# Attention over 512 heads: the row pitch of the spread V tile, 130 or 136 elements

## The chip, the cores and the metric

The kernel runs on one core of a Trainium2 chip. The metric is the device time of one execution in microseconds (us); before the change three runs gave 838.53, 837.74 and 838.30, a median of 838.3. A profiled execution of the same kernel took 837.31 us and has a span, from its first to its last instruction, of 835.6 us; all lines shown below come from it. The engines are named PE (TensorE's matmuls), PEld (TensorE's weight loads), ACT (ScalarE), DVE (VectorE), POOL (GpSimd) and SP (SyncE, which here issues all DMAs).

## The reference

Softmax attention without a mask, for 16 × 32 = 512 heads, each with 192 queries, 1024 keys and 128 dimensions, all in bf16:

```
scores = einsum("bhqd,bhkd->bhqk", q, k) * 128 ** -0.5
p      = softmax(scores, axis=-1)
out    = einsum("bhqk,bhkd->bhqd", p, v)
```

## The kernel before, in words

**Sets of four heads.** The 512 heads are worked on in 128 sets of four. A set is cut into three frames, so there are 384 frames. In frame `f = 3x + b` the tensor engine computes one third of the scores of set `x` (`qk(f)`, matmuls at L616) and then one third of the output of a set whose frame lies four back (`pv(f - LAG)`, matmuls at L638, `LAG` 4). That order, one score group and one PV group in turn, is written out in the loop at L666 to L671 and sets the beat of everything else.

**Scores.** The scores are made with keys on the partitions: a head's 1024 keys are 8 tiles of 128 keys, called `t`. Four heads sit at 32 partitions each and are multiplied side by side, one head on each quarter of the array's rows. A score group has 48, 64 or 48 matmuls. Its results lie in PSUM: head 0 in `f_s2`, heads 1 to 3 in `f_s0` or `f_s1` by turns.

**Exponential.** ACT reads a frame's scores from PSUM and writes exp(scale × score) as bf16 to `f_pt`, in two instructions: 512 wide for head 0 (L782) and 1536 wide for heads 1 to 3 (L785). No maximum is subtracted; at the end the row sums are tested for their range, and `_general_path` would do all of the work again if they lay outside. It is not executed here.

**V and its spread tile.** A set's V is loaded by one DMA of 1024 KB into `f_vs`, where each partition holds, for each of four heads, 8 rows of 128 elements without a gap. POOL copies them (function `spread`, L582, two copies per set with 16 rows each) into the tile `f_vp`, which has the shape 128 partitions × 2 sets × 32 rows × `VB` elements of bf16. Row `8·head + t` of a set is the right-hand side of the matmul for key tile `t` of that head. Only the first 128 elements of a row are written by the copy. Element 128 of each row is 1.0, since the whole tile is filled with ones at the start (L565). A matmul therefore reads 129 elements of a row, and the 129th column of its result is the row sum of the softmax:

```
return pe.matmul(
    O[m0: m0 + m, u, 0:129],
    pt[:, x % R, 2 * y + z, t * SQ + n0: t * SQ + n0 + m],
    vp[:, x % NVP, (2 * y + z) * T + t, 0:129],
```

The first operand after the output, a slice of 64 columns of `f_pt`, is loaded as weights; the row of `f_vp` streams through. Elements 129 up to `VB` of a row are never read.

**The order in a PV group.** A PV group has 32 matmuls: 16 pairs (`z` = 0, 1) that work side by side, the first on columns 0 to 63 of the array, the second on columns 64 to 127. The two of a pair read rows that are 8 rows apart, those of two neighbouring heads with the same `t`. In the first and second group of a set (`i` = 0, 1) there are two blocks, and each goes through `t` = 0 to 7, one row per pair. In the third group (`i` = 2) `t` is the outer loop and two output blocks (`u` = 0, 1) the inner one: each row is read by two pairs in succession, with other weights.

**Normalizing and storing.** After each PV group DVE takes the reciprocal of the row sums (L722) and multiplies the outputs by them into `f_ob` (L726). The next PV group waits for that, as there is one output bank, `f_o`. SP stores two sets with one DMA.

**K and Q.** K comes with a DMA of 1024 KB per set into `f_kn` (five buffers); DVE turns it in 32×32 blocks into `f_kx` (L701, three pieces per set), POOL reorders it into `f_kt` (L573), from which the score matmuls load their weights. Q comes with 192 KB per set and is turned by DVE (L710). On DVE these turns stand in one queue with the reciprocals and scalings: a K piece is turned five frames ahead of its use, right after the scaling of a frame.

**The loads.** SP issues per turn of its loop V of a set three ahead, K and Q of a set five ahead, and every second turn a store. A K load waits until DVE has turned the set that was in that buffer (L502), a V load until the PV groups of the set that was in that buffer are far enough (L516).

Of the kernel before, what the change touches and what calls it, by code (L numbers as in the profile page):

```python
# [408 lines left out]
def _attention_kernel(nc, q, k, v, out):  # L409
# [12 lines left out]
    NKN, NVS, NKT, NVP = 5, 5, 2, 2  # L422
    GQ = 2
    NSO = 3
    VB = 130

    qf = q.rearrange("b h s d -> (b h) s d")
    kf = k.rearrange("b h s d -> (b h) s d")
# [6 lines left out]
    with ExitStack() as outer:  # L435
# [27 lines left out]
        with ExitStack() as es:  # L463
            def sb(name, shape, dt):
                return es.enter_context(nc.sbuf_tensor(name, shape, dt))
# [13 lines left out]
            vs = sb("f_vs", [128, NVS, 4, T * D], BF16)  # L479
            vp = sb("f_vp", [128, NVP, 4 * T, VB], BF16)  # L480
            pt = sb("f_pt", [128, R, 4, T * SQ], BF16)
# [308 lines left out]
def bass_standalone__mha_softmax__near_ridge_kernel(  # L790
    nc: bass.Bass,
    q: bass.AP,
    k: bass.AP,
    v: bass.AP,
    out: bass.AP,
):
    _attention_kernel(nc, q, k, v, out)
# [28 lines left out]
```

## Time and profile before

| | us | share of the span of 835.6 us |
|---|---|---|
| PE busy (32926 matmuls) | 818.2 | 98% |
| PE, PV matmuls into `f_o` (L638, 12336) | 434.3 | |
| PE, score matmuls (L616, 20480) | 421.6 | |
| PEld busy | 726.0 | 87% |
| ACT busy | 748.6 | 90% |
| DVE busy | 599.3 | 72% |
| POOL busy | 550.0 | 66% |
| POOL, V copies (L582, 256 of 1.043 us) | 259.5 | |
| DMA, time of all packets over 16 engines | | 99.5% |

A group's busy time is the time in which at least one of its instructions was at work. Matmuls overlap, so the two groups of PE add up to more than PE's own total, and the mean of one matmul (222 ns in L638) is its way from start to end, not its share of the time; what a matmul costs is the distance from its start to the next one's. A row of the page ends with the idle time of the engine just ahead of the group's instructions and what ended most of it. In a list of waits the three numbers are the total in us, how many there were, and the longest. The line of GB/s has one number for each fortieth of the span.

The tile `f_vp` takes 2 × 32 × 130 × 2 = 16640 bytes of each partition. [...]

### The profile page before, as it was taken

What the parts mean: (1) busy time and instruction counts of PE and PEld (TensorE: products, weight loads), DVE (VectorE), ACT (ScalarE), POOL (GpSimd) and SP (SyncE); (2) the same over time, 40 slices, a digit from 0 to 9 for tenths busy, and PEclk for the clock granted to TensorE, in tenths of its full rate; (3) what the DMA queues carried; (4) which work ended last, traced back from release to release, by engine and by line L of the source; (5) the groups of instructions that cost most, each with busy time, mean ns of one, the idle gap of its engine ahead of it and who ended that gap; (6) DMA issues with size and microseconds to landing.
All of it is one profiled execution on the core that took longest, in us unless ns stands there. A gap on an engine that the chain in (4) does not pass through costs nothing. (4 is left out here: it accounts for less than half of the span.)

```text
span 835.6 us, 71554 instructions
## 1 busy us (share of the span) xinstructions
PE 818.2 (98%) x32926; PEld 726.0 (87%) x32926; DVE 599.3 (72%) x1288; ACT 748.6 (90%) x770; POOL 550.0 (66%) x646
## 2 busy tenths in 40 slices
PE   7899999999999999999999999999999999999995
PEld 5788888888888888888888888888888888888885
DVE  5577777777777777777777777777777777777763
ACT  5799999999999999999999999999999999999994
POOL 6566666666766766766766666666666666666670
PEclk9999999999999999999999999999999999999999
DMA  8999999999999999999999999999999999999941
GB/s 323 398 404 400 406 403 403 404 403 406 403 406 403 401 397 401 394 399 394 392 404 397 389 403 399 390 400 398 393 401 396 397 397 396 395 393 394 395 161 43
DMA packets 139213, 319.21 MB, mean 382 GB/s; under 512 B 7200, under 2 KB 57376, under 8 KB 122912
## 3 DMA queue, kind: packets, MB, share of 16 engines
q1 hardware_dynamic: 139168, 318.80, 99.5%
q14 instruction: 39, 0.32, 0.1%
q8 instruction: 6, 0.10, 0.1%
HBM read 293.60 MB, written 25.17 MB: 381 GB/s over the span
## 5 line engine op out<-in xcount | busy, mean ns | idle before, releaser
L785 ACT ACTIVATE f_pt<-f_s 128x1536 bf16<-128x1536 f32 x384 | 554.6, 1444 | 1.8 <-PE f_o L638 1.8
L573 POOL COPY f_kt<-f_kx 128x768 uint32<-128x768 uint32 (+1 forms) x384 | 293.8, 784 | 265.7 <-DVE f_kx L701 140.2
L638 PE MATMUL f_o<-f_vp,f_pt 128*64 128x129 bf16 x12336 | 434.3, 222 | 1.8 <-issue 1.8
L616 PE MATMUL f_s<-f_qt,f_kt 32*128 32x192 bf16 (+2 forms) x20480 | 421.6, 226 | 5.9 <-issue 3.4
L638 PEld LDWEIGHTS f_o<-f_vp,f_pt 128*64 128x64 bf16 x12336 | 373.9, 110 | 53.7 <-issue 23.5
L616 PEld LDWEIGHTS f_s<-f_qt,f_kt 32*128 32x128 bf16 x20480 | 347.6, 92 | 43.0 <-issue 6.5
L701 DVE STREAM_TRANSPOSE f_kx<-f_kn 128x768 uint32<-128x768 uint32 (+1 forms) x384 | 333.8, 870 | 10.1 <-DMA f_kn<-in_k_dram 10.1
L782 ACT ACTIVATE f_pt<-f_s 128x512 bf16<-128x512 f32 x384 | 229.3, 597 | 72.6 <-PE f_s L616 37.8
L582 POOL COPY f_vp<-f_vs 128x1024 uint32<-128x1024 uint32 x256 | 259.5, 1043 | 4.5 <-PE f_o L638 4.5
L722 DVE RECIPROCAL f_rinv<-f_o 128x2 f32<-128x2 f32 x381 | 65.0, 171 | 202.6 <-PE f_o L638 202.6
L726 DVE TENSOR_TENSOR f_ob<-f_o,f_rinv 128x256 bf16<-128x256 f32 x381 | 161.6, 424 | 13.3 <-DVE f_rinv L722 0.3
L710 DVE STREAM_TRANSPOSE f_qt<-f_qn 128x384 uint32<-128x384 uint32 x128 | 73.0, 570 | 0.0
L663 PE MATMUL f_o<-f_ones 128*128 128x512 bf16 x12 | 5.1, 610 | 1.1 <-POOL f_ones L564 1.1
L663 PEld LDWEIGHTS f_o<-f_ones 128*128 128x128 bf16 x12 | 1.7, 145 | 3.8 <-issue 2.7
L682 DVE MEMSET f_pt<- 128x3072 uint32 x1 | 2.6, 2618 | 1.5 <-PEq L811 1.5
L565 POOL MEMSET f_vp<- 128x4160 uint32 x1 | 3.6, 3569 | 0.0
L638 PE MATMUL f_s<-f_vp,f_pt 128*64 128x129 bf16 x96 | 3.1, 220 | 0.3 <-PEq L599 0.3
L638 PEld LDWEIGHTS f_s<-f_vp,f_pt 128*64 128x64 bf16 x96 | 2.9, 110 | 0.4 <-issue 0.4
L774 ACT ACTIVATE f_pt<-f_ones 128x3072 f32<-128x3072 bf16 x1 | 2.8, 2762 | 0.0
L774 ACT ACT_TABLE_LOAD x1 | 1.3, 1283 | 0.8 <-PEq L811 0.8
L722 DVE RECIPROCAL f_rinv<-f_s 128x2 f32<-128x2 f32 x3 | 0.5, 171 | 1.4 <-PE f_s L638 1.4
L676 PE MATMUL f_o<-f_bad,f_ones 128*1 128x1 bf16 x1 | 0.2, 165 | 1.3 <-DVEq L766 1.3
(13 smaller groups left out, 5.3 us busy)
## 6 DMA issues: line engine op xcount, KB each, us to landing
f_vs<-in_v_dram SPq DMA_DIRECT2D x128, 1024.0 KB, 10.5
f_kn<-in_k_dram SPq DMA_DIRECT2D x127, 1024.0 KB, 12.6
f_qn<-in_q_dram SPq DMA_DIRECT2D x128, 192.0 KB, 11.5
out_dram<-f_ob SPq DMA_DIRECT2D x63, 384.0 KB, 12.9
f_kn<-in_k_dram SPq DMA_DIRECT2D x1, 640.0 KB, 6.9
f_kn<-in_k_dram SPq DMA_DIRECT2D x1, 384.0 KB, 3.9
out_dram<-f_ob SPq DMA_DIRECT2D x2, 192.0 KB, 2.1
```

What stands on the lines that cost most here:

```text
L573: gp.tensor_copy(kt[:, x % NKT].bitcast(U32).rearrange("p U (j s u) c -> p U j s (u c)", s=2, u=2)[:, lo:hi], kx[:, x % 2].rearrange("p (U ...
L582: gp.tensor_copy(vp[:, x % NVP, 2 * T * i: 2 * T * i + 2 * T, 0:D].bitcast(U32), vs[:, x % NVS, 2 * i: 2 * i + 2, :].rearrange("p a (t d) ...
L616: ins = pe.matmul(S[:, c0: c0 + n1 - n0], kt[r, x % NKT, 2 * t + h, :, c], qt[r, x % R, h, n0:n1, c], start=w == 0 and g == 0, stop=w == 3 ...
L638: return pe.matmul(O[m0: m0 + m, u, 0:129], pt[:, x % R, 2 * y + z, t * SQ + n0: t * SQ + n0 + m], vp[:, x % NVP, (2 * y + z) * T + t, 0:129],
L663: pe.matmul(o_ps[:].rearrange("p a b -> p (a b)"), ones[:], ones[:].unsqueeze(1).to_broadcast([128, 4, 128]), start=True, stop=True)
L701: dve.transpose(kx[:, x % 2].rearrange("p (U s j u) -> p s u U j", s=2, j=32, u=2)[:, :, :, lo:hi], kn[:, x % NKN].rearrange("p (s u U i) ...
L710: dve.transpose(qt[:, x % R].bitcast(U32).rearrange("p b (y j u) c -> p u y b (j c)", y=3, u=2), qn[:, x % NKN].rearrange("p (u y b i) -> ...
L722: dve.reciprocal(ri, O[:, :, 128]).then_inc(s_rc, 1)
L726: dve.tensor_tensor(ob[:, so, 6 * a + 2 * w: 6 * a + 2 * w + 2, :], O[:, :, 0:128], ri.unsqueeze(2).to_broadcast([128, 2, D]), ALU.mult,). ...
L774: act.activation(pt[:, 1].rearrange("p a c -> p (a c)").bitcast(F32), ones[:, 0:1].to_broadcast([128, 2 * T * SQ]), ACT_FN.Copy).then_inc( ...
L782: act.activation(pt[:, x % R, 0, c], s1_ps[:], ACT_FN.Exp, scale=scale).then_inc(s_e1, 1)
L785: act.activation(pt[:, x % R, 1:4, c], s3_ps[f % 2][:], ACT_FN.Exp, scale=scale).then_inc(s_e3, 1)
```

## The change

`VB`, the number of elements from one row of `f_vp` to the next, goes from 130 to 136, that is, from 260 to 272 bytes. The 129 elements that are written and read in each row stay the same, as do the number and order of all instructions, their waits and the DMAs. The fill at the start covers 4352 words of 32 bits for each partition in place of 4160, and the tile takes 17408 bytes in place of 16640; `f_pt`, `f_ob` and the tiles after them lie 768 bytes higher.

```
     NKN, NVS, NKT, NVP = 5, 5, 2, 2
     GQ = 2
     NSO = 3
-    VB = 130
+    VB = 136
```

More of the change, by code (lines that the diff above doesn't have):

```diff
@@ L424, in _attention_kernel @@
     NSO = 3
-    VB = 130
+    VB = 136
     qf = q.rearrange("b h s d -> (b h) s d")
```

## Prediction, made before the changed kernel ran

> **What bounds the kernel now.** I read the page's engine totals first, then the costliest groups, then one stretch of the timeline, then the waits, and at the end the transfers.
>
> ```profile
> PE 818.2 (98%) x32926; PEld 726.0 (87%) x32926; DVE 599.3 (72%) x1288; ACT 748.6 (90%) x770; POOL 550.0 (66%) x646
> ...
> L573 POOL COPY f_kt<-f_kx 128x768 uint32<-128x768 uint32 (+1 forms) x384 | 293.8, 784 | 265.7 <-DVE f_kx L701 140.2
> L638 PE MATMUL f_o<-f_vp,f_pt 128*64 128x129 bf16 x12336 | 434.3, 222 | 1.8 <-issue 1.8
> L616 PE MATMUL f_s<-f_qt,f_kt 32*128 32x192 bf16 (+2 forms) x20480 | 421.6, 226 | 5.9 <-issue 3.4
> ...
> L582 POOL COPY f_vp<-f_vs 128x1024 uint32<-128x1024 uint32 x256 | 259.5, 1043 | 4.5 <-PE f_o L638 4.5
> ```
>
> The matmuls that read the spread V tile (L638) and those of the scores (L616) fill the span between them, with 1.8 and 5.9 us of idle time in front; POOL, which writes the tile, idles 265.7 us at L573 alone. The timeline of the matmuls alone shows the beat:
>
> ```profile
> 400.29 1.13 PE L638 MATMUL f_o<-f_vp,f_pt 128*64 128x129 bf16 x32
> 401.36 1.10 PE L616 MATMUL f_s<-f_qt,f_kt 32*128 32x192 bf16 x48
> 402.38 1.11 PE L638 MATMUL f_o<-f_vp,f_pt 128*64 128x129 bf16 x32
> 403.43 1.09 PE L616 MATMUL f_s<-f_qt,f_kt 32*128 32x192 bf16 x64
> 404.50 1.13 PE L638 MATMUL f_o<-f_vp,f_pt 128*64 128x129 bf16 x32
> 405.56 1.09 PE L616 MATMUL f_s<-f_qt,f_kt 32*128 32x128 bf16 x48
> ```
>
> Columns: start, length. A set of four heads is three score groups and three PV groups of 32, with no gap. By the first score matmul of each set, sets 3 to 127 follow each other every 6.295 and 6.285 us in turn, one exception at 6.371. Such a regular beat means that TensorE waits for nobody. So what a PV matmul costs is what counts.
>
> The waits and the transfers show who is next:
>
> ```profile
> DVE f_kx L701 <- DMA f_kn<-in_k_dram: 10.1, 5, 2.9
> ...
> GB/s 323 398 404 400 406 403 403 404 403 406 403 406 403 401 397 401 394 399 394 392 404 397 389 403 399 390 400 398 393 401 396 397 397 396 395 393 394 395 161 43
> ...
> q1 hardware_dynamic: 139168, 318.80, 99.5%
> ...
> f_kn<-in_k_dram SPq DMA_DIRECT2D x127, 1024.0 KB, 12.6
> ```
>
> Nobody waits for K after the start-up (five waits), yet the DMA engines are loaded 99.5% of the span, and a K transfer takes 12.6 us from issue to landing, two beats: there is always a backlog. DMA is a second bound just behind TensorE.
>
> [...] The trace has 56 ns for some pairs of PV matmuls (two run side by side) and 59 to 60 for the rest. [...] but the trace does follow the offset, below. [...] the trace moved 404 GB/s for 200 us[...].
>
> **The change, part by part.**
>
> *PV matmuls.* Row r of the tile starts at 260·r bytes now: at offset 0, 4, 8, 12 within 16 bytes as r mod 4 goes 0 to 3. Rows are numbered head·8 + t, so t = 0 and t = 4 begin at a multiple of 16 today. That is a test inside the trace. From the starts of single matmuls in 367 full PV groups between 20 and 800 us, the median from one pair to the next, in ns:
>
> ```
> pair of the group         1  2  3  4  5  6  7  8  9 10 11 12 13 14
> first group  (t = pair mod 8)  59 59 59 56 59 59 60 56 60 59 59 56 59 59
> second group (t = pair mod 8)  61 60 60 56 60 59 60 56 60 59 60 56 60 59
> third group  (t = pair div 2)  57 61 56 60 56 60 56 56 57 61 56 60 56 60
> ```
>
> (Pairs 0 and 15 border on the score groups, a switch of 80 to 185 ns.) In the first two groups exactly the pairs with t = 0 or 4 take 56 ns. In the third, where each row is read by two pairs in succession, the first reading takes 60 when the row is off the 16-byte grid and 56 when it is on it (pair 8, t = 4), the second reading 56 always. Offsets in the weights don't give this pattern: the first group's blocks start their weights 128 bytes apart and both show it. Why a second reading is free I can't say. With a pitch of 272 bytes all rows are on the grid, at 0, 16, 32 or 48 within 64 bytes, and rows at each of these places take 56 ns today.
>
> Saving: group one has 12 off-grid pairs at a mean of 59.6 against 56.3: 12 × 3.3 = 39.6 ns. Group two, 59.8: 12 × 3.5 = 42. Group three, six first readings at 60.0 against 55.9: 6 × 4.1 = 24.6. Sum 106 ns per set, from 6.290 to 6.184 us. Sets 0 to 2 are paced by K's and V's arrival at the start (starts at 6.9, 17.0, 30.2 us), so I count 125 sets: 13.2 us.
>
> *POOL's copies.* 256 at 1043 ns, now written at another pitch. The K copies fall from 859 to 635 ns over 256 words, 0.875 ns a word and 187 fixed; the V copy at that fixed part has (1043 − 187)/1024 = 0.836 ns a word. It is already the cheaper per word, so I take no change. Bounds: −100 to +100 ns each; POOL is idle a third of the time, and 200 ns per set more vanishes in L573's waits.
>
> *The first fill* (L565) grows from 4160 to 4352 words: 3569 × 4352/4160 = 3734, +165 ns. It ends at 4.5 us, POOL's next work starts at 5.80 and waits for DVE: hidden, nothing.
>
> *Later tiles* move up by 768 bytes, a multiple of 256: nothing. No instruction, wait or transfer is added.
>
> *ACT and DVE at the shorter beat.* ACT starts its 512-wide Exp at the end of each score group, the 1536-wide one 494 ns later, which takes 1444: 1.94 us out of a beat of 2.06. It fits. DVE idles 0.36 to 0.61 us ahead of each reciprocal; it fits.
>
> *DMA at the shorter beat.* A set moves 2.49 MB (K and V 1024 KB each, Q and output 192 each). Until 280 us the DMA ran at 404 GB/s, 6.16 us per set. What counts is the last of the 16 engines to land each K: set 12 at 77.2, 36 at 226.4, 126 at 791.0 us: 6.217 us per set, then 6.273. DVE's turn of a K starts this long after its landing: 5.98 us for set 12, 7.75 (36), 7.93 (60), 9.33 (126). TensorE will ask every 6.184. At set 12 about 0.8 us of slack has been eaten: 5.2 left. If the late engine keeps 6.217, the deficit over 114 sets is 3.8 us, less than the slack: nothing is lost. At 6.273 throughout, or as recorded, DVE begins to wait at about set 80 and the gain ends 3.3 to 3.5 us short. I take the middle, 6.245: 114 × 0.061 = 7.0 against 5.2, so 1.8 us is lost. DVE runs reciprocals and scalings in the same queue as the K turns, so its wait holds back the next PV group.
>
> Sum against the profiled span: 835.6 − 13.2 + 1.8 = 824.2. The other runs have a median of 838.3 (837.74 to 838.53); the same 11.4 off gives 826.9.
>
> **Rivals.** About 0.2% is what a measurement of this kernel tells from no change.
>
> 1. *DMA never binds.* Late landing engine at 6.217 or better; for it speaks 404 GB/s when all engines were loaded. Full saving: 838.3 − 13.2 = 825.1. Against: a backlog to the end, and the last engine at 6.273.
> 2. *DMA binds harder.* One slow engine of the recorded kind from the start, or transfers slowed by more overlap: half of the saving, 830 to 835. For: the rate falls from 404 to 396. Against: K's slack grew all the way.
> 3. *It doesn't do what it says.* The rhythm belongs to t, not to the address, and stays: 838.3. For: the free second reading, which I can't explain. Against: pair 8 of the third group.
> 4. *Slower.* The two matmuls of a pair read rows 8 apart, 2080 bytes today, 2176 after, a multiple of 128. If the streams then collide, each pair costs what an off-grid one does now. The fast ones of today (four pairs in groups one and two, nine in three) lose 3.4 to 4 ns: about 60 ns per set, 128 × 0.060 = 7.7: 846.0. It decides once a mean pair costs more than today's 58.6 ns. For: no such distance is in the trace. Against: weights read at a distance of 3072 bytes, also a multiple of 128, with nothing to see.
>
> **How the numbers follow.** Main case, saving with DMA taking back part, 825.9 to 829.5: 0.50. Rival 1, 823.5 to 825.9: 0.24. Rival 2: 0.11. Rival 3: 0.06. Rival 4: 0.09. Main and rival 1 hold 0.74; the range goes to 831 to take in part of rival 2: 823.5 to 831. Faster 0.50 + 0.24 + 0.11 = 0.85 and a little for a partial effect in rival 3: 0.86; same 0.05; slower 0.09.
>
> **What would show it.** Right: pairs of L638 at 56 ns for every t; PV groups of about 1.02 us from first start to next score group; sets at 6.18 us; more "DVE f_kx L701 <- DMA" waits, in the last third. POOL's L582 stays at 1043 ns. Wrong: 59 to 60 ns pairs still there (rival 3), or everywhere (rival 4); K waits from the first third on (rival 2).

## The result, and the profile after

The changed kernel takes 830.84 us (median of four runs, 829.76 to 831.68), the kernel before 838.02 on the same occasions (836.79 to 838.53): a ratio of 0.9916, 95% interval 0.9897 to 0.9934. So 7.2 us were gained, where 11.4 had been forecast (826.9 us; range 823.5 to 831.0).

The page of the changed kernel, the lines that answer to those shown of before, and the first fill:

```profile
PE 810.1 (98%) x32926; PEld 718.3 (87%) x32926; DVE 601.8 (73%) x1288; ACT 748.5 (90%) x770; POOL 550.9 (66%) x646
...
GB/s 323 399 403 399 406 403 401 406 403 402 405 403 404 402 400 389 399 382 374 398 400 398 376 399 395 388 400 405 387 383 399 406 397 397 387 393 405 399 323 46
...
q1 hardware_dynamic: 139168, 318.80, 100.6%
...
L638 PE MATMUL f_o<-f_vp,f_pt 128*64 128x129 bf16 x12336 | 424.9, 222 | 5.2 <-issue 3.3
...
L582 POOL COPY f_vp<-f_vs 128x1024 uint32<-128x1024 uint32 x256 | 259.9, 1044 | 5.9 <-PE f_o L638 5.5
...
L565 POOL MEMSET f_vp<- 128x4352 uint32 x1 | 3.7, 3730 | 0.0
...
f_kn<-in_k_dram SPq DMA_DIRECT2D x127, 1024.0 KB, 14.2
```

L638 is busy 9.4 us less (434.3 before), with the same mean of 222 ns: what shrank is the distance between starts. POOL's copy is unchanged. The timeline shows where the time came from:

```profile
301.41 1.10 PE L638 MATMUL f_o<-f_vp,f_pt 128*64 128x129 bf16 x32
302.44 1.10 PE L616 MATMUL f_s<-f_qt,f_kt 32*128 32x128 bf16 x48
303.47 1.10 PE L638 MATMUL f_o<-f_vp,f_pt 128*64 128x129 bf16 x32
304.50 1.09 PE L616 MATMUL f_s<-f_qt,f_kt 32*128 32x192 bf16 x48
305.52 1.10 PE L638 MATMUL f_o<-f_vp,f_pt 128*64 128x129 bf16 x32
306.55 0.49 PE L616 MATMUL f_s<-f_qt,f_kt 32*128 32x192 bf16 x20
```

From the start of a PV group to the next score group it is now 1.03 us in all three groups; before it was 1.06, 1.06 and 1.05 (medians 1059, 1063 and 1045 ns, now 1030 each). The starts of single pairs follow each other every 56 to 57 ns for every `t`. Sets follow each other every 6.20 and 6.22 us by turns, 6.210 on average against 6.290. That holds up to set 82. Then every second set is longer. The waits show two that were not there before:

```profile
DVE f_kx L701 <- DMA f_kn<-in_k_dram: 30.2, 42, 3.6
...
DVE f_ob L726 <- DMA out_dram<-f_ob: 7.1, 22, 0.9
```

DVE now waits 37 times for K after 480 us, and 22 times for an older store of the outputs, whose buffer it needs. One place, DVE's timeline first and TensorE's below it:

```profile
600.11 0.98 DVE L701 STREAM_TRANSPOSE f_kx<-f_kn 128x768 uint32<-128x768 uint32 x1 [0.20 <-DMA f_kn<-in_k_dram]
601.39 0.17 DVE L722 RECIPROCAL f_rinv<-f_o 128x2 f32<-128x2 f32 x1 [0.30 <-PE f_o L638]
602.42 0.42 DVE L726 TENSOR_TENSOR f_ob<-f_o,f_rinv 128x256 bf16<-128x256 f32 x1 [0.86 <-DMA out_dram<-f_ob]
```

```profile
601.29 1.10 PE L616 MATMUL f_s<-f_qt,f_kt 32*128 32x128 bf16 x48
602.99 1.10 PE L638 MATMUL f_o<-f_vp,f_pt 128*64 128x129 bf16 x32 [0.61 <-PEq L599]
```

K comes 0.20 us late, and the reciprocal behind it still starts on time: DVE had 0.30 us to spare. The scaling, however, waits 0.86 us for the store, and the PV group that needs its output bank starts 0.61 us late. Over the sets from 78 on, the odd ones, in which a store's buffer is taken up again, exceed the average of the sets before by 3.4 us in total, the even ones by 0.1. From set 76 on, 19 PV groups start more than 40 ns later after their score group than in the sets before, 3.2 us in all, and each of them follows a scaling that waited for a store. So it is the stores' late landing that costs TensorE time here, not K's.

### The profile page after: what moved, and what is told of

It reads as the page before. It is cut to its first block, busy times and chain, and to the rows that moved or that the text cites. A ratio compares the mean times of both kernels' runs of the same rounds, so it can differ in the third digit from the quotient of the medians.

```text
span 829.9 us, 71554 instructions
## 1 busy us (share of the span) xinstructions
PE 810.1 (98%) x32926; PEld 718.3 (87%) x32926; DVE 601.8 (73%) x1288; ACT 748.5 (90%) x770; POOL 550.9 (66%) x646
## 5 line engine op out<-in xcount | busy, mean ns | idle before, releaser
L785 ACT ACTIVATE f_pt<-f_s 128x1536 bf16<-128x1536 f32 x384 | 554.5, 1444 | 3.4 <-PE f_o L638 3.4
L638 PE MATMUL f_o<-f_vp,f_pt 128*64 128x129 bf16 x12336 | 424.9, 222 | 5.2 <-issue 3.3
L638 PEld LDWEIGHTS f_o<-f_vp,f_pt 128*64 128x64 bf16 x12336 | 366.1, 110 | 57.6 <-issue 28.3
L582 POOL COPY f_vp<-f_vs 128x1024 uint32<-128x1024 uint32 x256 | 259.9, 1044 | 5.9 <-PE f_o L638 5.5
L565 POOL MEMSET f_vp<- 128x4352 uint32 x1 | 3.7, 3730 | 0.0
L638 PE MATMUL f_s<-f_vp,f_pt 128*64 128x129 bf16 x96 | 3.1, 220 | 0.3 <-PEq L599 0.3
L638 PEld LDWEIGHTS f_s<-f_vp,f_pt 128*64 128x64 bf16 x96 | 2.8, 110 | 0.5 <-issue 0.5
## 6 DMA issues: line engine op xcount, KB each, us to landing
f_kn<-in_k_dram SPq DMA_DIRECT2D x127, 1024.0 KB, 14.2
f_qn<-in_q_dram SPq DMA_DIRECT2D x128, 192.0 KB, 12.9
out_dram<-f_ob SPq DMA_DIRECT2D x63, 384.0 KB, 13.8
```

What stands on the lines that cost most here:

```text
L582: gp.tensor_copy(vp[:, x % NVP, 2 * T * i: 2 * T * i + 2 * T, 0:D].bitcast(U32), vs[:, x % NVS, 2 * i: 2 * i + 2, :].rearrange("p a (t d) ...
L638: return pe.matmul(O[m0: m0 + m, u, 0:129], pt[:, x % R, 2 * y + z, t * SQ + n0: t * SQ + n0 + m], vp[:, x % NVP, (2 * y + z) * T + t, 0:129],
L785: act.activation(pt[:, x % R, 1:4, c], s3_ps[f % 2][:], ACT_FN.Exp, scale=scale).then_inc(s_e3, 1)
```

## The experiments

The kernel before, measured beside each, had medians of 837.45 to 838.15 us; the ratios are against it.

**1. All rows off the grid, at one place** (shift2). Pitch 272 bytes, but the row's data lie 4 bytes further on:

```
-    vp[:, x % NVP, 2 * T * i: 2 * T * i + 2 * T, 0:D]          # written by spread
+    vp[:, x % NVP, 2 * T * i: 2 * T * i + 2 * T, 2:2 + D]
-    vp[:, x % NVP, (2 * y + z) * T + t, 0:129],                # read by pv
+    vp[:, x % NVP, (2 * y + z) * T + t, 2:131],
```

> Pitch 272 bytes as in the changed kernel, but each row's 129 elements lie at elements 2 to 130 of its slot, so that every row begins 4 bytes past a multiple of 16. Theory A (what counts is whether a row begins on the 16-byte grid): all first readings of a row are off the grid, 40 pairs of each set of 48 against 30 in the kernel with pitch 260; at the 2.6 ns per such pair that the two traces give ((6.290 - 6.210) us / 30) a set takes 6.316 us and the kernel 841 us, up to 845 if it is 3.4 ns. Pairs in the trace at 59 to 60 ns for every t. Theory B (what counts is the distance between rows, 272 in place of 260 bytes, not where they begin): pairs at 57 ns and about 831 us, as in the changed kernel.

Measured 832.25 us, ratio 0.9935 (0.9914 to 0.9956). PV groups of 1030 ns, pairs at 56 to 57 ns, sets of 6.214 us up to set 77: TensorE works as in the changed kernel. Theory A, on which the forecast rested, is false: a row that begins off a multiple of 16 bytes costs nothing, as long as all do so by the same amount. POOL's copies took 1057 ns in place of 1044.

**2. Two places by turns, 0 and 8** (pitch132).

```
-    VB = 136
+    VB = 132
```

> Pitch of 132 elements, 264 bytes: rows with even t begin at a multiple of 16, rows with odd t 8 bytes past one. Theory A: 8 + 8 + 4 = 20 off-grid first readings per set in place of 30, 10 fewer: 26 ns per set less than the kernel with pitch 260, 6.263 us per set, 834.7 us; pairs at 57 ns for even t and 59 to 60 for odd t. That K arrives late costs little at this beat, at most 1 us. Theory B (distance): some other value for all t alike.

Measured 833.83 us, ratio 0.9961 (0.9949 to 0.9973). Even `t` 56 ns, odd `t` 59 to 60, groups of 1045, 1045 and 1038 ns, sets of 6.248 us. In the third group the first reading of an odd row took 61 ns, all else 56. By itself this would speak for theory A; with run 1 it says that a row's place counts only together with the row read before it.

**3 and 4. Half of the V traffic** (half_v_130 and half_v_136), on the kernels before and after:

```
-    vs[:, x % NVS, :, :],
-    vf[4 * x:4 * x + 4].rearrange("a (m t) d -> m a (t d)", t=T),
+    vs[:, x % NVS, 0:2, :],
+    vf[4 * x:4 * x + 2].rearrange("a (m t) d -> m a (t d)", t=T),
...
-    vs[:, x % NVS, 2 * i: 2 * i + 2, :]
+    vs[:, x % NVS, 0:2, :]
```

> The kernel before (pitch 130 elements) with half of the V traffic: only heads 0 and 1 of each set are loaded, and their V is used for heads 2 and 3 as well, so heads 2 and 3 get the wrong V. All engine instructions stay. Theory A' (TensorE sets the time of the kernel before, DMA does not): 838.0 us, within 0.2%, apart from up to 2 us gained in the first sets, which wait for their loads. Rival (DMA holds back the kernel before already): below 835 us.

> The changed kernel (pitch 136 elements) with the same half of the V traffic (heads 2 and 3 get the V of heads 0 and 1). Theory A' (in the changed kernel the late arrival of K takes back part of TensorE's saving): sets of 6.210 us from start to end, no wait for K after the start-up, 10.0 us below the same kernel with pitch 130 (125 sets of 0.080 us), so about 828 us or a little less. Rival (the rest of the forecast saving is missing on TensorE alone, and the waits for K cost nothing): 830.8 us, as in the changed kernel.

Measured 837.59 us with pitch 130 (ratio 0.9995, 0.9983 to 1.0006) and 827.40 with pitch 136 (0.9880, 0.9863 to 0.9897). The waits of the latter for loads and the beginning of its transfer line:

```profile
DVE f_kx L701 <- DMA f_kn<-in_k_dram: 7.7, 5, 3.2
...
f_kn<-in_k_dram SPq DMA_DIRECT2D x127, 1024.0 KB, 6.9
```

K lands in 6.9 us in place of 14.2, only the five waits of the start-up are left, none for a store, and the sets stay at 6.211 us to the end. So the kernel before is set by TensorE alone; the layout is worth 10.2 us on TensorE (837.59 − 827.40); and late transfers take back 3.4 of them (830.84 − 827.40; these two were measured on different occasions, and the trace gives 3.5, below).

**5. Another order of the rows, no other address** (t_order_130), on the kernel before:

```
-    for t in range(T):
+    for t in (0, 4, 1, 5, 2, 6, 3, 7):       # first and second group only
```

> The kernel before, pitch 130 elements, but in the first and second PV group of a set the key tiles are taken in the order 0, 4, 1, 5, 2, 6, 3, 7, so that each second row begins at the same place within 16 bytes as the one before it; no address in the tile is changed. Theory C (a pair costs more when its row begins at another place within 16 bytes than the row read before it, and not at place 0): 3 of 8 pairs of a block cost 59 to 60 ns in place of 6, the second reading of a place is as cheap as in the third group; 12 slow pairs fewer per set, 12 x 3.3 = 40 ns, sets of 6.25 us, 838 - 125 x 0.040 = 833 us. Theory A (a row off the 16-byte grid always costs more): 6 of 8 stay slow, 838 us.

Measured 834.59 us, ratio 0.9957 (0.9938 to 0.9976). Groups one and two fall to 1032 ns, the third stays at 1044; sets take 6.227 us until stores and K come late, which is below the 6.25 expected. Of the six steps up in a group only three or four are slow, at 58 to 60 ns. With the old pitch the order alone gives most of the gain on TensorE. Theory A is refuted a second time.

**6. The order turned round** (t_down_130), on the kernel before:

```
-    for t in range(T):
+    for t in range(T - 1, -1, -1):           # first and second group only; the accumulation
+                                             # then starts at t = T - 1 and stops at t = 0
```

> The kernel before, pitch 130 elements, but in the first and second PV group of a set the key tiles are taken from 7 down to 0: the places within 16 bytes go 12, 8, 4, 0, 12 and so on, a change at each pair as before, but down three times of four. No address in the tile is changed. Theory C1 (only a step up costs, 3 to 6 ns, and pairs can't go below 56 to 57 ns on average): groups one and two take 1.03 us as with pitch 136, sets of 6.22 to 6.23 us, 832 to 835 us with the waits for K. Theory C2 (any change to a place other than 0 costs): three of four pairs stay at 59 to 60 ns, groups of 1.06 us, sets of 6.29 us, 838 us.

Measured 832.48 us, ratio 0.9931 (0.9913 to 0.9948). Every pair reads another place than the pair before, but groups one and two take 1032 to 1033 ns, as theory C1 says. In their timeline they are the second and third L638 line, after one of the third group:

```profile
300.76 1.11 PE L638 MATMUL f_o<-f_vp,f_pt 128*64 128x129 bf16 x32
301.81 1.10 PE L616 MATMUL f_s<-f_qt,f_kt 32*128 32x192 bf16 x64
302.89 1.10 PE L638 MATMUL f_o<-f_vp,f_pt 128*64 128x129 bf16 x32
303.92 1.09 PE L616 MATMUL f_s<-f_qt,f_kt 32*128 32x128 bf16 x48
304.94 1.10 PE L638 MATMUL f_o<-f_vp,f_pt 128*64 128x129 bf16 x32
305.97 1.10 PE L616 MATMUL f_s<-f_qt,f_kt 32*128 32x192 bf16 x48
```

1.05 us for the third group, whose order was left, 1.03 for the other two. Within these only the pairs at a step up, from place 0 to 12, are slow, 60 to 61 ns: `t` = 3, which comes after `t` = 4, in each block, and `t` = 7, which opens the second block after `t` = 0. The steps down, from 12 to 8, 8 to 4 and 4 to 0, show 56 to 57 ns.

**7. Two places by turns, 0 and 4** (two_places), with a pitch on the grid:

```
-    vp = sb("f_vp", [128, NVP, 4 * T, VB], BF16)
+    vp = sb("f_vp", [128, NVP, 2 * T, 288], BF16)              # two rows in each 288
-    vp[:, x % NVP, (2 * y + z) * T + t, 0:129],
+    vp[:, x % NVP, ((2 * y + z) * T + t) // 2, 138 * (t % 2): 138 * (t % 2) + 129],
```

`spread` writes V to the same places; its lines are left out.

> A pitch that is on the 16-byte grid as in the changed kernel (576 bytes for each two rows), but with every second row 276 bytes after the one before it: rows of even t begin at place 0 within 16 bytes, rows of odd t at place 4. Theory C (a pair costs more when its rows begin at another place within 16 bytes than those read before, and not at place 0): slow pairs for odd t in the first and second PV group and at the first reading of an odd row in the third, 59 to 61 ns against 56 to 57, sets of about 6.247 us and 834 us, as with a pitch of 132 elements, where the second place is 8. Rival (it's the constant pitch of 260 bytes, or place 8, that costs): pairs at 57 ns for every t, 831 us.

Measured 832.00 us, ratio 0.9934 (0.9917 to 0.9950), not the 834 of theory C. Some pairs at a step up take 58 to 59 ns, but the others 56 to 57, and all three groups are 1030 ns as with one place. The eight steps up of a group, four in the third, cost it nothing.

**8. A pitch of 288 bytes** (pitch144).

```
-    VB = 136
+    VB = 144
```

> Pitch of 144 elements, 288 bytes: all rows at place 0 within 16 bytes as in the changed kernel, but each on a 32-byte multiple, and other distances between the rows that are read side by side (2304 bytes in place of 2176). Theory C: pairs at 57 ns, sets of 6.210 us until K comes late, 831 us, as in the changed kernel. Rival (distances between rows matter as such, or a grid of 32 bytes): other times for a pair.

Measured 834.51 us, ratio 0.9942 (0.9917 to 0.9966), with nine runs from 827.73 to 837.43. TensorE does as expected: groups of 1030 ns, sets of 6.214 us. The rest is lost in odd sets from 78 on, 6.4 us in the profiled run, with 26 waits for a store. The time of this one kernel scatters by 10 us between its runs; the kernel before on that occasion stayed within 835.67 to 839.00, and at half the V traffic, where nothing waits for K or a store after the start-up, the four runs of the changed kernel lay within 826.87 to 828.54 (run 4). So I put the scatter down to the late K and stores.

**9 to 11. What the width of the stream costs** (half V traffic, so that transfers don't matter):

```
-    O[m0: m0 + m, u, 0:129],
+    O[m0: m0 + m, u, 0:136],      # half_v_cols136; 0:128 in half_v_cols128, and
+                                  # 0:128 from elements 2:130 in half_v_cols128_shift2
```

The slice of `f_vp` changes in the same way. In the two kernels with 128, V's first 126 columns are copied and the reciprocal reads column 126.

Call a line, for counting, the 16 bytes from one multiple of 16 to the next. Theory D is a guess of mine: what a pair costs goes with the number of lines that its row touches. Its rival is that it goes with the number of elements. An estimate from the 56.6 ns that a pair takes in the changed kernel, with 17 lines and 129 elements: in proportion, a line would be 3.3 ns and an element 0.4.

> The changed kernel with half of the V traffic (heads 2 and 3 get the V of heads 0 and 1), and each PV matmul streams 136 elements in place of 129 (the last 7 are ones, and their results are not read). Theory D [...]: 136 elements touch the same 17 lines as 129, so pairs at 57 ns, sets at 6.21 us, 827 us as with 129. Rival [...] 845 us.

> The changed kernel with half of the V traffic (heads 2 and 3 get the V of heads 0 and 1), and each PV matmul streams 128 elements: V's first 126 columns and two ones, so the last two columns of each output are left out. Theory D: 16 lines in place of 17, [...] sets at 6.05 us, 827 - 125 x 0.16 = 807 us. Rival [...] sets at 6.19, 825 us.

> As the kernel with 128 streamed elements and half of the V traffic (last two output columns left out), but each row begins 4 bytes past a multiple of 16. Theory D: 128 elements now touch 17 lines, [...] 57 ns per pair, 827 us, as with 129 elements on the grid. Rival [...]: as the kernel with 128 elements on the grid.

Measured 843.35, 823.83 and 824.37 us (two runs each), sets of 6.334, 6.183 and 6.182 us; pairs at 59 to 60, 56, and 55 to 58 ns. Theory D fails three times: 136 elements cost 2.6 ns more than 129 though they touch the same 17 lines, and 128 elements cost the same whether they touch 16 lines or 17. The price goes with the number of elements: 3.4 ns more for the 8 from 128 to 136 (55.8 to 59.2), 0.42 each. In run 11 every third pair takes 57 to 58 ns and the two between 55, though all rows begin at one place, and the group takes 1017 ns as in run 10: a slow single pair need not cost the group anything.

**12. A sixth buffer for V** (vbuf6).

```
-    NKN, NVS, NKT, NVP = 5, 5, 2, 2
+    NKN, NVS, NKT, NVP = 5, 6, 2, 2
```

> The changed kernel with six buffers for V in place of five, so that SP, which issues V and K in one queue, waits for V's buffer one set less long, and a K load behind it is issued earlier. Theory E (in the last third the transfers themselves are the bound: the last of the 16 DMA engines has a backlog throughout): K is issued earlier and lands at the same pace, waits of DVE for K stay, 830 to 831 us. Rival (K comes late because SP holds its issue back behind V's): no waits for K after the start-up, sets of 6.210 us to the end, about 828 us.

Measured 833.45 us, ratio 0.9935 (0.9914 to 0.9956), in the profile:

```profile
DVE f_kx L701 <- DMA f_kn<-in_k_dram: 35.1, 50, 2.9
...
DVE f_ob L726 <- DMA out_dram<-f_ob: 10.4, 27, 0.8
```

All of the waits are still there, none fewer than in the changed kernel. But K was not issued earlier, which both theories expected of the sixth buffer. In sets 86 to 117 V's buffer is free 11.9 us before SP issues the load, in the changed kernel 5.6: there SP no longer waits for that buffer, and the sixth has nothing to shorten. SP issues K 12.3 us after K's own buffer is free (12.2 in the changed kernel), and issues of V, K and stores each follow the issue before them after 0.04 us. So the wait for V's buffer is not what holds K back. Whether SP's queue is, this run does not tell. This kernel and the changed one ran on different occasions, so the 2.6 us between them say little beside the scatter of run 8.

## Why the prediction was right or wrong

**What bounds the kernel: right.** Taking a fifth of the DMA traffic away from the kernel before changes nothing (run 3), and each change of the PV pairs moved its time.

**The PV pairs: the effect was there, its cause was not, and it was too large by a third.** The step that failed is the sentence that rows on the 16-byte grid cost 56 ns and rows off it 59 to 60. Run 1 put every row off the grid and lost nothing. Runs 5 and 6 left every address and changed only the order of the key tiles, and the groups that they changed fell from 1059 and 1063 ns to 1032 and 1033, close to the 1030 of the changed kernel. So what counts is which row is read after which.

I then took it that a step up costs, from a row's place within 16 bytes to a higher one (theories C and C1). The times of whole groups don't bear that out. That the unit is 16 bytes is read from the trace of before: there places 4, 8 and 12 take 59 to 61 ns at the first reading and place 0, four rows on, takes 56. Lines are 16 bytes again, as in runs 9 to 11. The table counts, in a group of 16 pairs, the steps up and the rows that begin in the very line in which the row ended that was read before them on the same columns of the array; both counts follow from the pitch and the order, with row 0 taken to begin at a multiple of 16. No trace gives that address; that `t` = 0 and 4 are the cheap ones fits it.

| PV group | steps up | rows that begin in the line where the row before ended | ns |
|---|---|---|---|
| before, first and second | 12 | 12 | 1059, 1063 |
| before, third | 6 | 6 | 1045 |
| pitch132, first and second | 8 | 8 | 1045 |
| pitch132, third | 4 | 4 | 1038 |
| t_order_130, first and second | 6 | 0 | 1032 |
| t_down_130, first and second | 3 | 0 | 1033 |
| two_places, first and second | 8 | 0 | 1030 |
| two_places, third | 4 | 0 | 1030 |
| after, shift2, pitch144, all | 0 | 0 | 1030 |

The third group of before and the first two of t_order_130 even go through the same places in the same order (0, 0, 4, 4, 8, 8, 12, 12), and take 1045 and 1032 ns. The time rises with the second count, if not in proportion (6 and 8 such rows both give 1045), and not with the first. This fits what the prediction left open, too: at a pitch of 260 bytes a row begins 2 bytes behind the end of the one before it, in the same line unless its own place is 0, as for `t` = 0 and 4; a second reading of a row goes back to the row's start, so it is free; and at 272 bytes each row begins a line of its own. So the change worked, though not by putting rows on a grid as such. This reading was found from the runs afterwards, and no run was made to test it. The 2 to 3 ns by which runs 5 and 6 stay above 1030, and why sharing a line should cost, stay open.

The size: 106 ns per set were summed, 80 came. The mis-sized term is the price of a cheap pair, which I took from pairs that stood beside dear ones: 55.9 and 56.3 ns. A stream of equal pairs doesn't hold that pace: in the changed kernel's first group the first four pairs are at 55.8 to 56.1 ns, the rest at 56.6 to 56.7, in the other groups mostly at 56.6 to 57.3. The 56 ns of before were in part a pair making good what the dear one had lost; in run 6 too the pairs between dear ones are at 55.8 to 56.3 ns. (The first group's own means come out of the trace nearer 59.2 and 55.9 than the 59.6 and 56.3 of the forecast, which moves its saving by 1 ns.) Over 48 pairs, 0.5 ns make 24 of the 26 ns that are missing. By width, with a weight load of its own for each matmul of a pair, a pair takes 55.8 to 56.3 ns at 128 columns, 56.6 to 57.3 at 129 and 59.2 to 59.6 at 136.

**POOL's copy, the fill, the later tiles: right.** 1044 ns in place of 1043; the fill took 3730 ns where 3734 were worked out; ACT's 1536-wide writes into `f_pt`, which lies 768 bytes higher, take 1444 ns as before, and DVE's scalings into `f_ob` 425 in place of 424. None of it is seen in the time.

**DMA: right that it takes part of it back, too small, and by another wait.** The case that I took, a K every 6.245 us, has DVE wait for K from about set 97 (5.2 / 0.061 sets after set 12), at a loss of 1.8 us; set 80 and 3.5 us belonged to the recorded course, and 6.273 throughout would have cost 4.9 (114 × 0.089 − 5.2), not 3.5. K's slack ran out sooner: 6.92 us at set 12, 5.24 at 36, 2.87 at 60, 0.81 at 72, 0.02 at 84. The pace at which the last engine lands K, one mis-sized term, was 6.34 us per set from set 36 to 84 and 6.30 from there to 120, at a beat of 6.210. But K's waits, 0.8 us at most in that stretch, mostly fit into DVE's idle time ahead of the reciprocal.

What holds TensorE back is the store, which I had not followed at all: with three output buffers the scaling that takes one up again waits for it, directly ahead of the next PV group. Its way from issue to landing has hardly grown (13.8 us on the page, 12.9 before). It is issued later. Of the 65 stores, the 41st to the 60th are issued 13.3 us after their last scaling, before the change 5.0, and land 0.1 us ahead of the reuse of their buffer, before the change 9.6. SP issues V, K, Q and stores one after another, and the issues themselves take longer. From the traces of before and after, the duration is the second number:

```profile
401.46 0.38 SPq L517 DMA_DIRECT2D f_vs<-in_v_dram  x1
401.88 3.59 SPq L503 DMA_DIRECT2D f_kn<-in_k_dram  x1
...
409.19 0.45 SPq L529 DMA_DIRECT2D out_dram<-f_ob  x1
```

```profile
589.21 3.71 SPq L517 DMA_DIRECT2D f_vs<-in_v_dram  x1
592.96 4.41 SPq L503 DMA_DIRECT2D f_kn<-in_k_dram  x1
...
600.38 2.24 SPq L529 DMA_DIRECT2D out_dram<-f_ob  x1
```

From 480 to 780 us an issue of V takes 2.0 us on average and one of K 3.0, before the change 0.4 and 1.4; issues fill 97% of SP's time, before 41%, at half the V traffic (run 4) 24%. An issue of K, of the same size, takes 0.5 us there. So it is the backed-up transfers that lengthen the issues and fill SP, and what SP issues late lands late. Which of the two sets the pace in the end, no run separates.

The rate in the page's slices falls from about 404 to 395 GB/s after some 280 us in both kernels. In the kernel before that is simply what is asked for: 2.49 MB in a set of 6.290 us are 396 GB/s, and from 360 to 780 us it moved 396. The changed kernel asks for 401 (6.210 us) and got 383 to 397 in stretches of 60 us from 300 to 780; why not more, stays open. Whether a fourth output buffer would bring back part of the 3.4 us was not tried; K's slack, which is used up too, speaks for less than all.

The sum in the profiled run: 835.6, later start of set 3 (37.4 us for 36.4) +0.9, TensorE 124 × 0.080 = −9.9, late sets +3.5: 830.1, against 829.9. By the runs: 10.2 gained on TensorE (forecast 13.2), 3.4 given back (1.8).

**The range: luck.** Both errors go the same way. The 830.84 us miss the stretch of the main case, 825.9 to 829.5, and lie 0.16 us inside the range, whose edge had been moved to 831 for another case, rival 2. The part given back also changes with the occasion: runs 1, 8 and 12, whose PV groups take 1030 ns as well, had medians of 832.25 to 834.51 us, above the range.

**The rivals.** DMA never binding: not so in the whole kernel; at half the V traffic that case occurs, at 827.4. DMA binding harder: the measured time lies in its 830 to 835, but its sign, waits for K from the first third on, did not come (from about 480 us), and the larger part of what is missing, 3.0 of 4.6 us, is missing on TensorE (13.2 − 10.2), not in the transfers (3.4 − 1.8). The rhythm belonging to `t` and not to the address: half true, since at a given pitch it belongs to the order of `t`. A collision of the two rows of a pair, 2176 bytes apart: none at 2176 nor at 2304 bytes (run 8), with groups of 1030 ns at both.

## What to carry to other kernels

If the trace of the kernel before already has instructions in the state that a change will bring, compare their starts; but look for the observation that the simple reading can't explain, and vary order and address separately before the cause is believed. Judge by the time of a whole group, since a slow single pair can be made good by its neighbours (run 11: 57 to 58 ns between pairs of 55, and the group 1017 as in run 10). The price read here from cheap pairs between dear ones, 55.9 and 56.3 ns, was too low against the 56.6 to 57.3 of a run of equal ones: take it from such a run. This kernel took 6.290 us per set where its transfers at 404 GB/s took 6.16, and 3.4 of the 10.2 us gained on the engine were paid back; so close to the pace of the transfers, each one that someone waits for has to be followed, stores included, from its issue on.

## What the runs showed of the hardware that was not expected

- Rows streamed one after another in pairs of matmuls side by side (129 bf16 elements): a group of 16 pairs takes 1030 to 1033 ns where no row begins in the same 16 bytes, from one multiple of 16 to the next, in which the row before it ended, and 1038, 1045, 1045 and 1059 to 1063 ns with 4, 6, 8 and 12 such rows. That this sharing of 16 bytes is the cause fits all runs, but was not tested by itself.
- A start 4 bytes off a multiple of 16 costs nothing as such: 1030 ns for a group of 16 pairs either way (runs after and 1).
- Cost by width: 56 ns a pair for 128 elements, 57 for 129, 59 to 60 for 136; whether the row of 128 begins at a multiple of 16 bytes or 4 bytes past one doesn't count (823.8 and 824.4 us).
- The DMA engines moved 404 GB/s from 60 to 240 us, before and after the change. In the changed kernel K took 14.2 us to land (median), and one issue of a K load held SP for 3.0 us on average (480 to 780 us), against 0.5 at half the V traffic.
